# A filter by Fourier transform with a two-layer network behind it: the exchange between partition quarters by copy and add, arrays read back 32 steps ahead, tables loaded in another order

## Chip, cores and metric

The kernel runs on one core of one Trainium2 chip. The metric is the device time of one execution in microseconds; lower is better.

## What is computed

```python
X = np.fft.rfft(x, axis=1)                       # x: 8 x 3008 x 256, float32
Y = X * (filt_r + 1j * filt_i)[None]             # filters: 1505 x 256
y = np.fft.irfft(Y, n=3008, axis=1)
h = y.reshape(24064, 256) @ w_in                 # 256 x 2048
g = np.maximum(h, 0) + alpha * np.minimum(h, 0)  # alpha: 2048
out = g @ w_out                                  # 2048 x 256, float32
```

## The kernel before

**The work.** Each of the eight batches is filtered along its 3008 rows, and each row of the result goes through the network. The transform of 3008 points is done as 94 x 32 by matmuls with constant tables, in fp16. For batch b (class `Fft`) the pieces are:

- `piece_a` (L148), eight of them: the 94-point transform of a quarter tile of x (`xs`), evicted by ScalarE (ACT) to `asb`. `save_a` (L159) writes `asb` to `a_dram`.
- `turn_a` (L163): reads `a_dram` back as `at`, with the other index on the partitions (the "array" of the change). There is one `at`.
- `piece_b` (L172), six: the 32-point transform into `psF`. Its partitions hold, in quarters of 32, real and imaginary parts. The product with the complex filter is made by two multiplies on VectorE (DVE): `ww` is the product with the filter whose quarters are exchanged and signed (`filts_s`), `uu` that with the plain one (`filt_s`). Then `ww` of the neighbouring quarter has to be added to `uu`: four DMAs on GpSimd's (POOL's) queue with `accum_op=add`, one for each quarter (L189), which is the exchange.
- `piece_c` (L192), six: the inverse 32-point transform of `uu`, evicted by ACT to `v`. After every second one `turn_c` (L207) writes a third of `v` to `v_dram`, and the last one reads it back as `zt` in four DMAs.
- `pair_d` (L235), eight: the inverse 94-point transform into `yT`, the network's input.

The network runs over 48 blocks of 512 rows (four of 384), each in 16 steps. A step j does `up(j)`: 128 of the 2048 hidden units, two matmuls; after every odd j ACT evicts two of them to `gtb` (L458), DVE forms the negative part (L461), and after every fourth DVE adds it (L463, 128 x 2048). In the same step `prev.down(j)` does a sixteenth of the block before's second product (L480). So the loop has 768 steps, and the first block has no `down`.

**The order is written by hand.** `plan` maps a step to functions, which are issued ahead of that step's `up`. `plan_fft` (L494) takes for each batch the steps of its `piece_a`, `turn_a`, x loads, `piece_b`, `piece_c` and `pair_d`. For batches three to seven the steps count from p = 96 (b - 1): the last `piece_a` at p - 48 or p - 50, `turn_a` at p - 20, `piece_b` at p + 2, p + 14, ..., p + 62, `piece_c` at p + 14 to p + 74, `pair_d` from p + 91. Each engine takes its instructions in this order. SyncE's (SP's) queue carries the saves, the reads back and the output stores, POOL's the x loads and the exchange.

**Buffers.** `uu` has three, `ww` two, `psF` one of two PSUM banks, `hps` and `op` two each.

**Batch 0** is done ahead of the loop by class `First` (L253), without a way through DRAM: transposes on TensorE (PE) instead. Its filter rows for the first piece stand in `fst`, loaded by SP; the other filters are loaded by POOL. Tables are `twf`, `twi`, `twx` (three parts of the constants), `wf1`, `wi3` and the signs `sgn`. Matmuls of the identity (`warm`) fill PE's idle time there. Of batch 0's four groups of 752 rows the first is finished ahead of the loop, the other three in its first 30 steps (`piece_t`, a transposition into `zt`, and `pair_d`).

Of the kernel before, what the change touches and what calls it, by code (L numbers as in the profile page):

```python
# [9 lines left out]
FP16 = mybir.dt.float16  # L10
# [3 lines left out]
N1 = 94  # L14
N2 = 32
NK = 24
D = 256
# [4 lines left out]
OP = mybir.AluOpType  # L22
# [28 lines left out]
def kernel(  # L51
# [22 lines left out]
    p_uw = ctx.enter_context(tc.tile_pool(name="p_uw", bufs=2))  # L74
# [33 lines left out]

    def load_x(b, c):
        xs = p_x.tile([N1, 8 * D], FP16, name="xs")  # L110
        for r in (slice(0, 48), slice(48, N1)) if b else (slice(0, N1),):
            nc.gpsimd.dma_start(out=xs[r], in_=xrow(b, c)[r])  # L112
        return xs

    def load_filt(eng, dst, ha, hb):
        n = hb - ha
        for i, src in enumerate((filt_r, filt_i)):
            for e in range(2):
                q = 64 * e + 32 * i
# [18 lines left out]
    class Fft:  # L138
# [30 lines left out]
                        out=self.at[q : q + N2, ka:kb],  # L169
                        in_=a_dram[self.b, r + ka : r + kb].rearrange("k s d -> s k d"))  # L170

        def piece_b(self, q):  # L172
            psf = banks(False)
            for h in range(2):
                for par in range(2):
                    r = slice(64 * par, 64 * par + 64)
                    for e in range(2):
                        k = 4 * q + 2 * h + e
                        nc.tensor.matmul(psf[64 * e : 64 * e + 64, par, 256 * h : 256 * h + 256],  # L179
                                         twf_s[r, k], self.at[r, k], start=True, stop=True)  # L180
            px = psf.rearrange("p r (h d) -> p r h d", h=2)
            uu = p_uw.tile([128, 2, 2, D], FP16, name="uu", bufs=3)
            ww = p_uw.tile([128, 2, 2, D], FP16, name="ww")
            fs, f = (t[:, 2 * q : 2 * q + 2].rearrange("p h r d -> p r h d") for t in (filts_s, filt_s))
            nc.vector.tensor_mul(ww, px, fs)  # L185
            nc.vector.tensor_mul(uu, px, f)  # L186
            for o in range(0, 128, 32):
                i = o ^ 32
                nc.gpsimd.dma_start(out=uu[o : o + 32], in_=ww[i : i + 32], accum_op=OP.add)  # L189
            self.uw[q] = uu  # L190

        def piece_c(self, q):  # L192
            if q == 0:
                self.v = p_fft.tile([128, NK, D], FP16, name="v")
                self.zt = p_fft.tile([96, N2, D], FP16, name="zt")
            u = self.uw.pop(q)
            ps = psH.tile([128, 2, 512], FP32, name="hps")
            for h in range(2):
                for e in range(2):
                    r = slice(64 * e, 64 * e + 64)  # L200
                    for par in range(2):
                        nc.tensor.matmul(ps[64 * par : 64 * par + 64, e, 256 * h : 256 * h + 256],  # L202
                                         twi_s[r, 4 * q + 2 * h + par], u[r, par, h], start=True, stop=True)
            on_act(self.v[:, 4 * q : 4 * q + 4].rearrange("p (h e) d -> p e h d", e=2),
                   ps.rearrange("p e (h d) -> p e h d", h=2))
# [134 lines left out]
    def tables(eng, names, ka, kb):  # L340
        for n, t in (("twf", twf_s), ("twi", twi_s), ("twx", twx_s)):
            if n in names:
                eng.dma_start(out=t[:, ka:kb], in_=consts[n].ap()[:, ka:kb])

    xc = {(0, c): load_x(0, c) for c in range(4)}
    f0 = First()
    tables(nc.sync, ("twf",), 0, 8)
    nc.sync.dma_start(out=al16, in_=moe_alpha.rearrange("(j p) -> j p", p=128))
    nc.sync.dma_start(out=id32, in_=id32_d.ap())
    nc.sync.dma_start(out=sgn_s, in_=sgn_d.ap())  # L350
    nc.sync.dma_start(out=wf1_s, in_=consts["wf1"].ap())
    nc.sync.dma_start(out=wi3_s, in_=consts["wi3"].ap())
    load_filt(nc.gpsimd, filt_s, 1, 4)
    load_filt(nc.gpsimd, filt_s, 4, 8)
    load_filt(nc.gpsimd, filt_s, 8, 12)
# [9 lines left out]
    def warm(n, kind="o"):  # L365
        pw = bank(kind)
        for _ in range(n):
            nc.tensor.matmul(pw[:, 0:128], id16, id16, start=True, stop=True)
# [22 lines left out]
    for kp in range(0, 12, 2):  # L391
        if kp < 10:
            f0.piece_b(kp + 2)
            f0.piece_b(kp + 3)
        f0.piece_c(kp)
        f0.piece_c(kp + 1)
        f0.keep_c(kp, both if kp == 10 else (on_act, on_act))
        if kp < 6:
            f0.turn_at(kp + 6, 2, on_act)
        elif kp < 10:  # L400
            warm(4, "f")
# [6 lines left out]
    warm(8, "f")  # L408
# [82 lines left out]
    def put(step, fn, *args):  # L491
        plan.setdefault(step, []).append((fn, args))

    def plan_fft(b, a_at, ta, quarters, x_at, b_at, c_at, d_at):  # L494
# [12 lines left out]
        for q in range(6):  # L507
            put(b_at[q], f.piece_b, q)
        for q in range(6):
            put(c_at[q], f.piece_c, q)  # L510
            front.add(c_at[q])
            if q % 2 == 1:
                put(c_at[q] + 1, f.turn_c, q // 2)
        for i in range(8):
            put(d_at[i], f.pair_d, i, on_act)

    for g, ts, ds in ((1, (1, 3), (6, 8)), (2, (12, 14), (17, 19)), (3, (22, 24), (27, 29))):
        for i in range(2):
            put(ts[i], f0.piece_t, 2 * g + i, both[i])
            put(ds[i], f0.pair_d, 2 * g + i, both[i])  # L520
# [7 lines left out]
    def d_steps(p):  # L528
        return [p + t for t in (91, 93, 104, 108, 116, 120, 140, 152)]

    plan_fft(1, (8, 10, 12, 14, 16, 18, 20, 22), 24, 4, (12, 16, 20, 24), (32, 38, 46, 52, 58, 64),
             (46, 52, 58, 64, 70, 76), (90, 92, 98, 101, 106, 116, 136, 146))
    plan_fft(2, (54, 60, 66, 72, 80, 84, 88, 94), 97, 4, (62, 74, 86, 96), range(110, 170, 10),
             range(120, 180, 10), d_steps(96))
    for b in range(3, NB):
        p = 96 * (b - 1)
        a_at = (10, 16, 22, 28, 32, 38, 42, 48) if b == 3 else (6, 10, 18, 22, 30, 34, 42, 46)
# [53 lines left out]
```

## Time and profile before

| | |
|---|---|
| median of 3 runs | 813.55 us (811.96 to 815.87) |
| the profiled execution | 813.39 us, span 811.6 us |
| mean granted clock of PE | 0.976 |
| busy PE / DVE / ACT / POOL | 777.0 / 576.3 / 582.6 / 185.0 us |
| DMA traffic | 100.67 MB, mean 124 GB/s |

The span is the time from the first to the last instruction of the profiled execution; 1.8 us lie around it. PE is TensorE's matmuls, PEld its weight loads. A row of instructions in order of time has the start and the length in us, then the engine, the line of the kernel, the operation, out<-in with shapes and the count, and in brackets the engine's idle time just before and what ended it. A row of waits has the waiting engine and line, what it waited for, and then the sum in us, the number and the longest. L245 and L248 are the helpers `on_act` and `on_dve`, which evict for many pieces, so they are told apart by the tiles.

### The profile page before, as it was taken

The page shows a single profiled execution, that of the slowest core. Times are in us where ns is not written, and L with a number is a line of the kernel's source. Part 1 is how long each engine was busy: PE and PEld are TensorE (multiplying, and loading weights), DVE is VectorE, ACT ScalarE, POOL GpSimd, SP SyncE. Part 2 cuts the span into 40 slices and gives each one's busy share as a digit, 9 for nine tenths or more (in the row PEclk, how much of TensorE's full clock was granted, in tenths as well). Part 3 has the DMA queues.
Part 4 walks back from the last instruction along what each step waited for, and adds up shares of the span by engine and source line. Part 5 has one row for each costly group of instructions (what it writes and reads, how often), then busy time and mean ns, then how long its engine had stood idle before and what let it go on. Part 6 is the DMA issues. An engine that isn't in the chain of part 4 may idle for free.

```text
span 811.6 us, 16322 instructions
## 1 busy us (share of the span) xinstructions
PE 777.0 (96%) x6497; PEld 521.0 (64%) x6497; DVE 576.3 (71%) x1079; ACT 582.6 (72%) x667; POOL 185.0 (23%) x267
## 2 busy tenths in 40 slices
PE   6788999999999999899999999989999999999998
PEld 5555667665665666666666666756666666676666
DVE  3667886677765787677776778658776887767664
ACT  2587688877765877588776887668877677676764
POOL 5421450143302431033311243013130322100000
PEclk7699999999998999999999999999999999999999
DMA  8988588677594764957658665765449444531111
GB/s 157 196 193 187 120 157 208 178 127 140 97 186 97 133 146 80 200 85 144 129 110 161 123 127 122 155 122 101 103 74 194 83 76 87 110 86 34 40 40 53
DMA packets 97325, 100.67 MB, mean 124 GB/s; under 512 B 11216, under 2 KB 82400, under 8 KB 97056
## 3 DMA queue, kind: packets, MB, share of 16 engines
q1 hardware_dynamic: 80368, 70.25, 34.4%
q0 software_dynamic: 16880, 29.38, 26.4%
q8 instruction: 51, 0.84, 0.4%
q14 instruction: 26, 0.21, 0.1%
HBM read 55.28 MB, written 46.66 MB: 126 GB/s over the span
## 4 chain that ended last, share of the span: by engine, by line
PE 73%; DMA 16%; SPq 3%; ACT 3%; DVE 2%; POOL 1%; issue 1%; DVEq 0%; ACTq 0%; POOLq 0%
PE hps L449 33%; PE op L480 33%; DMA at<-a_dram 8%; DMA xs<-in_x_dram 4%; PE hps L155 2%; PE psF L224 2%; PE psF L179 2%; SPq L168 2%; DMA v_dram<-v 1%; DMA uu<-ww 1%; PE hps L202 1%; ACT gtb L458 1%; SPq L219 1%; DMA filt_s<-in_filt_i_dram 1%; DMA win_s<-in_moe_w_in_dram 1%
## 5 line engine op out<-in xcount | busy, mean ns | idle before, releaser
L458 ACT ACTIVATE gtb<-hps 128x1024 f16<-128x1024 f32 (+1 forms) x384 | 386.0, 1005 | 156.1 <-PE hps L449 154.2
L449 PE MATMUL hps<-yT,win_s 128*128 128x512 f16 (+1 forms) x1536 | 438.1, 377 | 2.5 <-ACT gtb L458 1.3
L480 PE MATMUL op<-wout_s,gtb 128*128 128x256 f16 x3008 | 438.8, 274 | 0.1
L480 PEld LDWEIGHTS <-gtb 128*128 128x128 f16 x3008 | 295.0, 98 | 171.9 <-issue 4.5
L461 DVE TENSOR_SCALAR m<-gtb,alm_s 128x512 f16<-128x512 f16 (+1 forms) x768 | 233.1, 347 | 186.5 <-ACT gtb L458 185.3
L463 DVE TENSOR_TENSOR gtb<-gtb,m 128x2048 f16<-128x2048 f16 (+1 forms) x192 | 231.1, 1203 | 10.4 <-PE hps L449 0.5
L189 POOL DMA_DIRECT2D uu<-ww x168 | 134.2, 1199 | 418.0 <-PE hps L449 179.3
L449 PEld LDWEIGHTS <-win_s 128*128 128x128 f16 x1536 | 143.3, 98 | 62.9 <-issue 16.4
L245 ACT ACTIVATE asb<-hps 96x1024 f16<-96x1024 f32 x56 | 57.1, 1020 | 11.2 <-PE hps L155 11.0
L485 ACT ACTIVATE osb<-op 128x512 f32<-128x512 f32 (+1 forms) x97 | 56.2, 579 | 5.3 <-issue 2.8
L185 DVE TENSOR_TENSOR ww<-psF,filts_s 128x1024 f16<-128x1024 f32 x42 | 51.2, 1219 | 8.6 <-PE psF L179 8.6
L245 ACT ACTIVATE v<-hps 128x1024 f16<-128x1024 f32 x42 | 43.0, 1024 | 17.7 <-PE hps L202 17.5
L245 ACT ACTIVATE yT<-psF 128x752 f16<-128x752 f32 x59 | 47.0, 797 | 8.4 <-PE psF L224 8.3
L112 POOL DMA_DIRECT2D xs<-in_x_dram x60 | 37.1, 708 | 66.7 <-PE hps L155 57.1
L186 DVE TENSOR_TENSOR uu<-psF,filt_s 128x1024 f16<-128x1024 f32 x42 | 51.1, 1216 | 0.0
L155 PE MATMUL hps<-xs,wf_s 94*96 94x512 f16 x112 | 33.4, 379 | 0.1
L224 PE MATMUL psF<-wi_s,zt 96*128 96x94 f16 x500 | 31.4, 206 | 1.5 <-DVE zt L248 1.5
L179 PE MATMUL psF<-at,twf_s 64*64 64x256 f16 x336 | 19.7, 288 | 12.7 <-DMA at<-a_dram 12.7
L224 PEld LDWEIGHTS <-zt 96*128 96x128 f16 x512 | 29.1, 99 | 4.3 <-issue 2.3
L179 PEld LDWEIGHTS <-twf_s 64*64 64x64 f16 x336 | 6.9, 105 | 22.7 <-DMA at<-a_dram 12.5
L202 PE MATMUL hps<-uu,twi_s 64*64 64x256 f16 x336 | 17.4, 272 | 2.8 <-DMA uu<-ww 2.7
L293 DVE TENSOR_TENSOR uu<-hps,filt_s 128x1024 f16<-128x1024 f32 x11 | 12.8, 1219 | 4.2 <-PE hps L289 3.6
(58 smaller groups left out, 155.4 us busy)
## 6 DMA issues: line engine op xcount, KB each, us to landing
out_dram<-osb SPq DMA_DIRECT2D x160, 128.0 KB
a_dram<-asb SPq DMA_DIRECT2D x28, 384.0 KB
uu<-ww POOLq DMA_DIRECT2D x168, 64.0 KB, 3.4
v_dram<-v SPq DMA_DIRECT2D x84, 128.0 KB
zt<-v_dram SPq DMA_DIRECT2D x28, 384.0 KB
at<-a_dram SPq DMA_DIRECT2D x20, 384.0 KB
xs<-in_x_dram POOLq DMA_DIRECT2D x28, 192.0 KB, 4.4
xs<-in_x_dram POOLq DMA_DIRECT2D x28, 184.0 KB, 5.4
```

Of the source, the lines that this page charges most:

```text
L155: nc.tensor.matmul(ps[0:96, u], wf1_s, xs[:, o : o + 512], start=True, stop=True)
L185: nc.vector.tensor_mul(ww, px, fs)
L186: nc.vector.tensor_mul(uu, px, f)
L189: nc.gpsimd.dma_start(out=uu[o : o + 32], in_=ww[i : i + 32], accum_op=OP.add)
L224: nc.tensor.matmul(ps[:, m], self.zt[:, 8 * g + 4 * mh + m, dh * 128 : dh * 128 + 128], wi3_s, start=True, stop=True)
L245: nc.scalar.activation(o, i, AF.Copy)
L449: nc.tensor.matmul(self.hps[:, j % 2, 0:tn], win_s[:, kt, j * 128 : (j + 1) * 128], yT[:, kt, self.t0 : self.t0 + tn], start=(kt == 0), st ...
L458: nc.scalar.activation(g[:, 2 * i : 2 * i + 2], self.hps[:, :, 0:tn], AF.Copy)
L461: nc.vector.tensor_scalar(m[:, 2 * i + h], g[:, 2 * i + h], 0.0, a, OP.min, OP.mult)
L463: nc.vector.tensor_add(g, g, m)
L480: nc.tensor.matmul(self.op[:, si - s0], self.gts[k][:, 128 * si : 128 * si + 128], wout_s[:, k], start=(si == s0 and k == 0), stop=(si == ...
L485: nc.scalar.activation(osb[:, 0:m], self.op[:, 0:m], AF.Copy)
```

## The change

- **The exchange.** For batch one it stays. For batches two to seven the four POOL DMAs are plain copies of `ww` into a new tile `sw`, and a new piece `piece_s` adds `sw` to `uu` on DVE, seven steps (batch two) or eight steps (later ones) after `piece_b`.
- **The reads back.** `turn_a` of batches three to seven moves from p - 20 to p - 32. `piece_b` stays at p + 2 and after, so the reads are 34 steps ahead of the first one and about 32 ahead of the group of steps that begins at p. For batches one and two the whole plan is shifted: batch one's `piece_a` by four steps later, its `piece_b` from 32 to 36, its `piece_c` to 12 steps after each `piece_b`; batch two's `turn_a` from 97 to 92, its `piece_b` from 110 to 104 on.
- **Tables and loads ahead of the loop.** `fst` is the first load of SP; `twi` and `twx` of the first eight columns come ahead of the first loop. The later tables, `wi3`, `wf1` and `sgn` are loaded in that loop, held back by a small memset of `twf_s` on DVE after its sixth piece. The x tiles of batch 0 are loaded in halves.
- **Warm matmuls** are a quarter as many, each four times as wide.
- **Batch 0's groups.** Group one is done in halves in steps 0 to 9, in `op`'s buffers; groups two and three move a few steps later, the one evicted by DVE, the other by ACT.

```diff
     def load_x(b, c):
-        for r in (slice(0, 48), slice(48, N1)) if b else (slice(0, N1),):
+        for r in (slice(0, 48), slice(48, N1)) :
...
-        def piece_b(self, q):
+        def piece_b(self, q, direct):
...
+            sw = None if direct else p_uw.tile([128, 2, 2, D], FP16, name="sw")
...
             for o in range(0, 128, 32):
                 i = o ^ 32
-                nc.gpsimd.dma_start(out=uu[o : o + 32], in_=ww[i : i + 32], accum_op=OP.add)
-            self.uw[q] = uu
+                if direct:
+                    nc.gpsimd.dma_start(out=uu[o : o + 32], in_=ww[i : i + 32], accum_op=OP.add)
+                else:
+                    nc.gpsimd.dma_start(out=sw[o : o + 32], in_=ww[i : i + 32])
+            self.uw[q] = uu, sw
+
+        def piece_s(self, q):
+            uu, sw = self.uw[q]
+            nc.vector.tensor_add(uu, uu, sw)
...
+    load_filt(nc.sync, f0.fst, 0, 1)
     tables(nc.sync, ("twf",), 0, 8)
...
-    nc.sync.dma_start(out=sgn_s, in_=sgn_d.ap())
-    nc.sync.dma_start(out=wf1_s, in_=consts["wf1"].ap())
-    nc.sync.dma_start(out=wi3_s, in_=consts["wi3"].ap())
+    tables(nc.sync, ("twi", "twx"), 0, 8)
...
-            nc.tensor.matmul(pw[:, 0:128], id16, id16, start=True, stop=True)
-    warm(36)
+            nc.tensor.matmul(pw.rearrange("p (r c) -> p r c", r=4), id16,
+                             id16.unsqueeze(1).to_broadcast([128, 4, 128]), start=True, stop=True)
+    warm(9)
     for i in range(8):
...
-            warm((16, 8, 8, 8)[i // 2])
-        if i == 3:
-            nc.vector.memset(f0.fst[:, :, :, 0:1], 0.0)
-            load_filt(nc.sync, f0.fst, 0, 1)
-            tables(nc.sync, ("twi", "twx"), 0, 8)
+            warm((4, 2, 2, 2)[i // 2])
+        if i == 5:
+            nc.vector.memset(twf_s[:, 8:24, 0:1], 0.0)
             tables(nc.sync, ("twf", "twi", "twx"), 8, 24)
-        if i == 5:
+            nc.sync.dma_start(out=wi3_s, in_=consts["wi3"].ap())
+            nc.sync.dma_start(out=wf1_s, in_=consts["wf1"].ap())
+            nc.sync.dma_start(out=sgn_s, in_=sgn_d.ap())
...
         for q in range(6):
-            put(b_at[q], f.piece_b, q)
+            put(b_at[q], f.piece_b, q, not add)
+            if add:
+                put(b_at[q] + add, f.piece_s, q)
...
-    for g, ts, ds in ((1, (1, 3), (6, 8)), (2, (12, 14), (17, 19)), (3, (22, 24), (27, 29))):
+    for i in range(4):
+        put(i, f0.half_t, 4 + i, both[i % 2], "o")
+        put(6 + i, f0.half_d, 4 + (0, 2, 1, 3)[i], both[i % 2], "o")
+    for g, ts, ds, evict in ((2, (13, 15), (21, 23), on_dve), (3, (25, 27), (31, 33), on_act)):
...
-    plan_fft(1, (8, 10, 12, 14, 16, 18, 20, 22), 24, 4, (12, 16, 20, 24), (32, 38, 46, 52, 58, 64),
-             (46, 52, 58, 64, 70, 76), (90, 92, 98, 101, 106, 116, 136, 146))
-    plan_fft(2, (54, 60, 66, 72, 80, 84, 88, 94), 97, 4, (62, 74, 86, 96), range(110, 170, 10),
-             range(120, 180, 10), d_steps(96))
+    plan_fft(1, range(12, 28, 2), 28, 4, (17, 21, 25, 29), range(36, 72, 6), 0, range(48, 84, 6),
+             (91, 93, 98, 101, 106, 116, 136, 152))
+    plan_fft(2, (50, 56, 62, 68, 74, 80, 84, 88), 92, 4, (57, 69, 81, 89), (104, 114, 126, 136, 148, 158), 7,
+             (114, 126, 136, 148, 158, 170), d_steps(96))
...
-        plan_fft(b, a_at, p - 20, 1, [a_at[2 * c + 1] + 2 for c in range(4)],
-                 range(p + 2, p + 74, 12), range(p + 14, p + 86, 12), d_steps(p))
+        plan_fft(b, a_at, p - 32, 1, [a_at[2 * c + 1] + 2 for c in range(4)],
+                 range(p + 2, p + 74, 12), 8, range(p + 14, p + 86, 12), d_steps(p))
```

More of the change, by code (lines that the diff above doesn't have):

```diff
@@ L195, in piece_c @@
                 self.zt = p_fft.tile([96, N2, D], FP16, name="zt")
-            u = self.uw.pop(q)
+            u, _ = self.uw.pop(q)
             ps = psH.tile([128, 2, 512], FP32, name="hps")
@@ L400 @@
         elif kp < 10:
-            warm(4, "f")
+            warm(1, "f")
     nc.gpsimd.dma_start(out=filt_s[:, 0:1], in_=f0.fst)
@@ L407 @@
         nc.gpsimd.dma_start(out=filt_s[o : o + 32], in_=filt_s[o - 32 : o])
-    warm(8, "f")
+    warm(2, "f")
     for i, (evict, kind) in enumerate(((on_act, "o"), (on_dve, "o"), (on_act, "f"), (on_dve, "h"))):
@@ L492, in put, with plan_fft @@
         plan.setdefault(step, []).append((fn, args))
-    def plan_fft(b, a_at, ta, quarters, x_at, b_at, c_at, d_at):
+    def plan_fft(b, a_at, ta, quarters, x_at, b_at, add, c_at, d_at):
         f = Fft(b)
@@ L515, in plan_fft @@
             put(d_at[i], f.pair_d, i, on_act)
-    for g, ts, ds in ((1, (1, 3), (6, 8)), (2, (12, 14), (17, 19)), (3, (22, 24), (27, 29))):
+    for i in range(4):
+        put(i, f0.half_t, 4 + i, both[i % 2], "o")
+        put(6 + i, f0.half_d, 4 + (0, 2, 1, 3)[i], both[i % 2], "o")
+    for g, ts, ds, evict in ((2, (13, 15), (21, 23), on_dve), (3, (25, 27), (31, 33), on_act)):
         for i in range(2):
-            put(ts[i], f0.piece_t, 2 * g + i, both[i])
-            put(ds[i], f0.pair_d, 2 * g + i, both[i])
+            put(ts[i], f0.piece_t, 2 * g + i, evict)
+            put(ds[i], f0.pair_d, 2 * g + i, evict)
     def neg(ha, hb):
@@ L529, in d_steps @@
         return [p + t for t in (91, 93, 104, 108, 116, 120, 140, 152)]
-    plan_fft(1, (8, 10, 12, 14, 16, 18, 20, 22), 24, 4, (12, 16, 20, 24), (32, 38, 46, 52, 58, 64),
-             (46, 52, 58, 64, 70, 76), (90, 92, 98, 101, 106, 116, 136, 146))
-    plan_fft(2, (54, 60, 66, 72, 80, 84, 88, 94), 97, 4, (62, 74, 86, 96), range(110, 170, 10),
-             range(120, 180, 10), d_steps(96))
+    plan_fft(1, range(12, 28, 2), 28, 4, (17, 21, 25, 29), range(36, 72, 6), 0, range(48, 84, 6),
+             (91, 93, 98, 101, 106, 116, 136, 152))
+    plan_fft(2, (50, 56, 62, 68, 74, 80, 84, 88), 92, 4, (57, 69, 81, 89), (104, 114, 126, 136, 148, 158), 7,
+             (114, 126, 136, 148, 158, 170), d_steps(96))
     for b in range(3, NB):
         p = 96 * (b - 1)
-        a_at = (10, 16, 22, 28, 32, 38, 42, 48) if b == 3 else (6, 10, 18, 22, 30, 34, 42, 46)
+        a_at = (10, 16, 22, 28, 34, 36, 44, 48) if b == 3 else (6, 10, 18, 22, 30, 34, 42, 46)
         a_at = [p - 96 + t for t in a_at]
-        plan_fft(b, a_at, p - 20, 1, [a_at[2 * c + 1] + 2 for c in range(4)],
-                 range(p + 2, p + 74, 12), range(p + 14, p + 86, 12), d_steps(p))
+        plan_fft(b, a_at, p - 32, 1, [a_at[2 * c + 1] + 2 for c in range(4)],
+                 range(p + 2, p + 74, 12), 8, range(p + 14, p + 86, 12), d_steps(p))
     prev = None
```

## Prediction

> **What bounds the kernel now.** I read the page first, then the list of waits, then PE's instructions in order of time at the waits, then windows of 16 us around them.
>
> ```profile
> PE 777.0 (96%) x6497; PEld 521.0 (64%) x6497; DVE 576.3 (71%) x1079; ACT 582.6 (72%) x667; POOL 185.0 (23%) x267
> ...
> PEclk7699999999998999999999999999999999999999
> ```
>
> PE is busy 96% of the span, DVE and ACT some 70%. So PE sets the time, and what can be won is the time in which PE waits, and the time in which it runs with a low granted clock. The clock row (tenths, 40 slices of 20 us) shows such slices at the start and one near 244 us. The list of waits names the waiters:
>
> ```profile
> DVE m L461 <- ACT gtb L458: 185.3, 202, 3.1
> ...
> PE psF L179 <- DMA at<-a_dram: 12.7, 8, 3.0
> ...
> PE hps L202 <- DMA uu<-ww: 2.7, 2, 1.9
> ```
>
> PE's longest waits are those of `piece_b` (L179) for `at`, the read back of the first transform's array; then those of `piece_c` (L202) for `uu`, the exchange of the partition quarters. The 185.3 us of DVE are slack: DVE idles there until ACT has written the next `gtb`. PE's instructions in order of time (start, length, then in brackets the idle time before) put the L179 waits at one place of each batch, the first `piece_b`:
>
> ```profile
> 80.35 0.41 PE L179 MATMUL psF<-at,twf_s 64*64 64x256 f16 x6 [0.68 <-DMA at<-a_dram]
> ...
> 242.22 0.30 PE L179 MATMUL psF<-at,twf_s 64*64 64x256 f16 x2 [0.25 <-DMA at<-a_dram]
> ...
> 245.12 0.64 PE L179 MATMUL psF<-at,twf_s 64*64 64x256 f16 x6 [2.60 <-DMA at<-a_dram]
> ...
> 343.10 0.57 PE L179 MATMUL psF<-at,twf_s 64*64 64x256 f16 x6 [2.98 <-DMA at<-a_dram]
> ...
> 439.37 0.41 PE L179 MATMUL psF<-at,twf_s 64*64 64x256 f16 x6 [1.75 <-DMA at<-a_dram]
> ...
> 534.52 0.64 PE L179 MATMUL psF<-at,twf_s 64*64 64x256 f16 x6 [3.00 <-DMA at<-a_dram]
> ...
> 629.91 0.41 PE L179 MATMUL psF<-at,twf_s 64*64 64x256 f16 x6 [0.97 <-DMA at<-a_dram]
> ```
>
> The windows around these places (length, then busy time of PE, PEld, DVE, ACT, POOL with counts, granted clock, DMA share, GB/s), with one from the first block of the main loop:
>
> ```profile
> 48.00:64.00 16.00, 14.26 (x102) 8.31 (x102) 13.08 (x26) 14.83 (x16) 6.12 (x12) 1.00 0.86 207
> 240.00:256.00 16.00, 13.15 (x81) 7.58 (x79) 8.36 (x16) 7.57 (x10) 3.14 (x4) 0.79 0.56 99
> 336.00:352.00 16.00, 13.00 (x89) 7.70 (x86) 9.53 (x20) 8.62 (x11) 3.15 (x4) 0.89 0.75 131
> 432.00:448.00 16.00, 14.26 (x115) 9.61 (x114) 11.29 (x20) 10.77 (x13) 3.14 (x4) 1.00 0.76 130
> 528.00:544.00 16.00, 12.97 (x88) 7.91 (x86) 9.68 (x18) 8.83 (x11) 3.14 (x4) 0.89 0.71 122
> 624.00:640.00 16.00, 15.03 (x125) 10.04 (x123) 12.01 (x22) 10.42 (x14) 3.14 (x4) 1.00 0.76 136
> ```
>
> In three of the five the clock fell as well, and 81 to 89 matmuls ran instead of 115 to 125. So a wait here costs twice: the wait itself, and PE's slow time behind it.
>
> The sum below is made against the profiled execution, 813.39 us for a span of 811.6; the median of the runs shown is 813.55, so nothing has to be shifted.
>
> **The reads of `at`, batches three to seven.** They are issued at step p - 32 instead of p - 20, and the first `piece_b` stays at p + 2. The waits are 0.25 + 2.60 + 2.98 + 1.75 + 3.00 + 0.97 = 11.6 us (PE's idle time in the five windows gives 2.85 + 3.00 + 1.74 + 3.03 + 0.97 = 11.6 too). The clock costs (0.21 + 0.11 + 0.11) x 16 = 6.9 us of full-speed time. Together 18.5 us; I take off 1.0, since some of the slow time lies inside the waits and is counted twice: 17.5. Do twelve steps suffice? Where the reads stand now, in SP's queue and in the chain of waits:
>
> ```profile
> 223.25 3.85 DMA v_dram<-v
> ...
> 231.15 13.93 DMA at<-a_dram
> ```
>
> ```profile
> 228.94 9.16 SPq L168 DMA_DIRECT2D at<-a_dram  x4
> ```
>
> SP issues them right behind `turn_c(2)`, which at step p - 21 writes `v_dram` and reads `zt` back, so the `at` reads share the DMA engines with the `zt` reads and end at 245.1, 16 us after the first issue. Twelve steps earlier they stand ahead of `turn_c(2)`. A step is about 1 us (768 steps lie within the span of 811.6), so the shift is 11 us or a little more against a longest wait of 3.0: 8 us in hand. Two things can hold SP: the array must be written (last `save_a` at p - 48 or p - 50, 16 steps before), and `at` must be free (`piece_b(5)` of the batch before at p - 34, two steps before). Neither reaches the next use. Queued behind the four issues on SP are the output stores and, eleven steps later, `turn_c(2)`; SP was held 9.16 us by these issues with the `zt` reads in front, and eleven steps are about as long, so `zt` is not later than now. What comes next in turn is the exchange of `piece_b(5)`, at p - 34, which now runs beside the reads; see the next part. Bounds: 11.6 (the waits alone) to 18.5.
>
> At this place the Trainium skill speaks for a smaller gain: "TensorE: Matmul & The Clock Gate", section "HAM oscillation", gives as the rule that only idle gaps over about 3.4 us take the clock away. By it none of these waits costs clock, the term would be 11.6 and the time 6 us later. The trace differs: after waits of 2.6 to 3.0 us the windows show 0.79 and 0.89, after 1.75 and 0.97 us 1.00.
>
> **Copy and add instead of the accumulating DMA, batches two to seven.** Removed is the wait of the four POOL issues for the second multiply. Added are 36 `tensor_add` of 128x1024 on DVE, each waiting for four landings, and everything on DVE queues behind that wait. One steady piece in order of time on DVE, and POOL's four issues:
>
> ```profile
> 274.34 1.22 DVE L185 TENSOR_TENSOR ww<-psF,filts_s 128x1024 f16<-128x1024 f32 x1
> ...
> 281.90 0.61 DVE L461 TENSOR_SCALAR m<-gtb,alm_s 128x512 f16<-128x512 f16 x2
> 284.01 0.62 DVE L461 TENSOR_SCALAR m<-gtb,alm_s 128x512 f16<-128x512 f16 x2 [1.50 <-ACT gtb L458]
> ...
> 286.33 1.22 DVE L185 TENSOR_TENSOR ww<-psF,filts_s 128x1024 f16<-128x1024 f32 x1
> ```
>
> ```profile
> 276.98 3.18 POOL L189 DMA_DIRECT2D uu<-ww  x4 [5.88 <-DVE uu L186]
> ```
>
> The window around it, an L463 for the length of an add, and the time from issue to landing of the 168 exchange DMAs:
>
> ```profile
> 272.00:288.00 16.00, 16.00 (x134) 10.31 (x132) 13.04 (x24) 13.08 (x16) 4.26 (x6) 1.00 0.82 176
> ```
>
> ```profile
> L463 DVE TENSOR_TENSOR gtb<-gtb,m 128x2048 f16<-128x2048 f16 (+1 forms) x192 | 231.1, 1203 | 10.4 <-PE hps L449 0.5
> ```
>
> ```profile
> DMA to landing us min/median/max: 2.4/3.4/6.1
> ```
>
> The add is half an L463: about 0.65 us, 36 of them 23 us of DVE. POOL now waits for the second multiply, which starts when the first ends and is as long; without that wait it can start 1.1 us sooner, at 275.9. Four issues take 3.18, the last begins near 278.2 and lands 3.4 later, at 281.6. The add is put eight steps behind `piece_b`, where j is 2, 6, 10 or 14, that is between the first and the second pair of L461 of a group: here at 282.5, where DVE idles 1.50 us. So it finds its data and fits into the gap, and is done at 283.2; `piece_c` follows the next `piece_b`, near 286, 2.8 us later. Cost nothing, the cover being that gap. Without it a piece costs the add, at most 0.65 x 36 = 23 us if DVE were the bound, which at 71% it is not. For batch two the add stands seven steps behind and `piece_c` ten to twelve. Now all its `piece_c` stand ten behind and waited 2.7 us in two of them; the copy starts 1.1 us sooner and gives 0.65 back. I take half of the 2.7 as saved, 1.4; bounds -2 and +2.7. For the sixth piece of each batch, beside the reads of `at`, a landing of 6.1 us would bring the add to 284.3 and its end to 285, still ahead of `piece_c`. Nothing is taken for it.
>
> **First block of the loop.** In 48 to 64 us ACT is busy 14.83 of 16: there ACT is the bound, since no down projection runs yet.
>
> ```profile
> L245 ACT ACTIVATE asb<-hps 96x1024 f16<-96x1024 f32 x56 | 57.1, 1020 | 11.2 <-PE hps L155 11.0
> ...
> L245 ACT ACTIVATE yT<-psF 128x752 f16<-128x752 f32 x59 | 47.0, 797 | 8.4 <-PE psF L224 8.3
> ...
> L245 ACT ACTIVATE zt<-psF 96x1024 f16<-96x1024 f32 x3 | 3.0, 1017 | 2.0 <-PE psF L324 2.0
> ...
> L245 ACT ACTIVATE zt<-op 96x512 f16<-96x512 f32 x1 | 0.6, 593 | 1.0 <-PE op L324 1.0
> ...
> L245 ACT ACTIVATE yT<-op 128x376 f16<-128x376 f32 x1 | 0.5, 484 | 0.1
> ```
>
> Out of steps 0 to 15 on ACT go two `asb` (batch one's `piece_a` starts at 12 instead of 8), two `zt` and one `yT`: 2.04 + 2.03 + 0.80 = 4.9 us. In come two half `zt` and two half `yT`: 2.2. Net 2.7 us less. DVE, busy 13.1 of the 16 already, takes over group two's `zt` and may become the bound itself; the lower bound is then less than half of this, 1.2 us. Block two gets two `asb` more, beside PE work that is as long. Batch one's `at` wait (0.68 above) keeps its distance of ten steps and stays. In favour of more: group two's evictions no longer alternate, and DVE's waits there go. I take 3.0; bounds 1.2 to 4.5.
>
> **Before the loop.** The single filter rows (`fst`) and `twi`, `twx` now load ahead of the first x tiles' end, and x comes in eight DMAs instead of four. The longer warm matmuls have the same columns in a quarter of the instructions.
>
> ```profile
> fst<-in_filt_r_dram SPq DMA_DIRECT2D x4, 32.0 KB
> ...
> twi_s<-c_twi SPq DMA_DIRECT2D x1, 128.0 KB
> ```
>
> ```profile
> PE psF L368 <- issue: 2.3, 1, 2.3
> ```
>
> With `filt_i` and `twx` these are 8 x 32 + 2 x 128 = 512 KB; at the 207 GB/s of the window above 2.5 us of the DMA engines, which x may lose at most, and nothing if they fit beside it. On the other side 69 pairs of PE instructions go; PE's 2.3 us without any recorded wait may be instructions that came late, and may go or move. The ends are +2.5 and -2.3; I take 0, the middle. But one call of `warm`, the last, keeps its count of 4 and so gets four times as long, and stands right ahead of the last pieces before the loop:
>
> ```profile
> 40.89 0.63 PE L368 MATMUL op<-id 128*128 128x128 f16 x4
> ...
> 41.31 0.52 PE L224 MATMUL hps<-wi_s,zt 96*128 96x94 f16 x4
> ```
>
> Four take the 0.42 us between these starts, so sixteen take 1.7. The pieces behind them waited for `zt` only little, so up to 1.3 us is added, and nothing where the eviction of `zt` hides it: +0.8.
>
> The sum: 813.4 - 17.5 - 1.4 - 3.0 + 0.8 = 792.3 us.
>
> **The rivals.** First, half of the gain comes back: the next arrival at the head of a batch is late. For it: the exchange of the sixth piece now meets four 384 KB reads, and `zt` waits behind them on SP. Against it: the 2.8 us and the 8 us in hand. If each of five batches gives back 2 us, the time is 802.
>
> Second, and slower: the add blocks DVE. A piece has 12.0 us of DVE time (274.34 to 286.33), of which (16 - 13.04) / 16, 2.2 us, are idle by the window around it, so 1.5 us is left behind the add. Landing L us after the last issue, the add waits L - 4.3 (278.2 + L against 282.5), and DVE falls behind by L - 5.8 in each of 36 pieces. The gain of 21.1 is eaten from L = 6.4 on; at L = 7 the time is 792.3 + 36 x 1.2 = 835. For it: 6.1 occurs today. Against it: that is the largest of 168, the median is 3.4, and only one piece in six runs beside the reads.
>
> Third, the change doesn't do what it says: SP is held at the earlier place and the reads start no sooner. Then only 3.6 us of the other parts are left: 810. For it: SP's queue is in order, and the reads wait for a `piece_b` only two steps before. Against it: 30 steps remain after that.
>
> **How the numbers follow.** A measurement of this kernel tells about 0.5% from no change, here 4 us. The forecast has 0.64, with 785 to 797 as its own range from the bounds of the start (+3.8, -2.3), of block one (1.2 to 4.5) and batch two; the first rival has 0.19, the second 0.11, the third 0.06. The range takes in the forecast and the first rival, 785 to 806. Faster is the forecast and the first rival, 0.83; the third lies at the edge and stands for no change, 0.06; slower is the second, 0.11.
>
> **What would show it.** Right: no L179 wait for `at` after 200 us and a clock of 1.00 in the windows that follow; the new add's group with 36 of about 0.65 us and little idle time before them for the landing of `sw`; L461's idle time down by about 23 us; the first block shorter by 3 us. Wrong: L202 waiting for the add, L224 waiting for `zt` at the head of a batch, DVE idle ahead of the add by more than 1.5 us a piece, or a first step of the loop that begins more than 2.5 us later than now.

## The result, and the profile after

| | median | runs |
|---|---|---|
| before | 812.91 us | 811.96 to 815.87 (4) |
| changed | 793.15 us | 792.41 to 793.86 (4) |

The ratio is 0.9751, 95% interval [0.9723, 0.9779]: faster by 2.5%. The forecast was 792.3 us. The profiled execution of the changed kernel took 792.9 us for a span of 791.1, at a mean granted clock of 0.989 (0.976 before).

In the changed kernel lines have moved down by eight: ACT's `gtb` is L466, DVE's negative part L469, `up` L457, `down` L488, the matmuls of `piece_c` L210 (L202 before) and those of `pair_d` L232 (L224 before). The multiplies are L186 (`ww`) and L187 (`uu`), the accumulating exchange L191, the copy L193, the add L198. Busy time and the clock row on its page, and the rows of the groups that the change touches:

```profile
PE 768.3 (97%) x6428; PEld 512.9 (65%) x6428; DVE 596.7 (75%) x1117; ACT 582.9 (74%) x669; POOL 142.9 (18%) x271
...
PEclk8799999999999999999999999999999999999999
...
L193 POOL DMA_DIRECT2D sw<-ww x144 | 70.8, 500 | 385.1 <-DVE ww L186 382.3
...
L198 DVE TENSOR_TENSOR uu<-uu,sw 128x1024 f16<-128x1024 f16 x36 | 24.6, 684 | 0.0
```

DVE has 20 us more to do and the kernel is 20 us faster. The add does not wait: no idle time stands before it (0.0 in its row). An exchange issue on POOL takes 0.50 us; the accumulating one took 1.20, as its row on the page of before shows:

```profile
L189 POOL DMA_DIRECT2D uu<-ww x168 | 134.2, 1199 | 418.0 <-PE hps L449 179.3
```

Then the changed kernel's list of waits, and the windows that stand against the five of before (length; busy PE, PEld, DVE, ACT, POOL; clock; DMA share; GB/s):

```profile
PE psF L232 <- DVE uu L187: 3.1, 3, 1.2
...
PE psF L179 <- DMA at<-a_dram: 1.3, 2, 0.7
```

```profile
240.00:256.00 16.00, 16.00 (x139) 10.54 (x137) 13.63 (x24) 12.77 (x15) 3.37 (x7) 1.00 0.46 99
...
528.00:544.00 16.00, 16.00 (x144) 10.48 (x142) 13.79 (x23) 13.92 (x17) 2.52 (x6) 1.00 0.35 94
```

The waits for `at` fell from 12.7 us to 1.3, both of those left lie in batch two, and PE is busy throughout at full clock in these two windows, where it ran at 0.79 and 0.89.

Where the time went can be read from the starts of ACT's `gtb` evictions. Those of steps 0 and 96, then 192 and 672, first in the trace of before, then in the changed kernel's:

```profile
45.43 1.01 ACT L458 ACTIVATE gtb<-hps 128x1024 f16<-128x1024 f32 x1
...
144.82 1.02 ACT L458 ACTIVATE gtb<-hps 128x1024 f16<-128x1024 f32 x1 [0.26 <-PE hps L449]
...
241.58 1.02 ACT L458 ACTIVATE gtb<-hps 128x1024 f16<-128x1024 f32 x1 [0.22 <-PE hps L449]
...
718.05 1.02 ACT L458 ACTIVATE gtb<-hps 128x1024 f16<-128x1024 f32 x1 [0.33 <-PE hps L449]
```

```profile
43.53 1.02 ACT L466 ACTIVATE gtb<-hps 128x1024 f16<-128x1024 f32 x1 [0.65 <-PE hps L457]
...
141.13 1.02 ACT L466 ACTIVATE gtb<-hps 128x1024 f16<-128x1024 f32 x1 [0.33 <-PE hps L457]
...
240.08 1.02 ACT L466 ACTIVATE gtb<-hps 128x1024 f16<-128x1024 f32 x1 [0.22 <-PE hps L457]
...
697.48 1.02 ACT L466 ACTIVATE gtb<-hps 128x1024 f16<-128x1024 f32 x1 [0.33 <-PE hps L457]
```

| stretch | before | changed | difference | predicted |
|---|---|---|---|---|
| start to step 0 | 45.43 | 43.53 | -1.9 | +0.8 |
| step 0 to 96 | 99.39 | 97.60 | -1.8 | -3.0 |
| step 96 to 192 (beside it, batch two) | 96.76 | 98.95 | +2.2 | -1.4 |
| step 192 to 672 (batches three to seven) | 476.47 | 457.40 | -19.1 | -17.5 |

So the total agrees to a microsecond, three terms do not, and what made the fourth had still to be found. The experiments use the same four points. Each stretch is read from one profiled execution, and 31 runs of the kernel before lie between 806.49 and 818.66 us; so a difference of 2 or 3 us in one stretch counts for little unless a wait in the trace accounts for it.

### The profile page after: what moved, and what is told of

Same layout as the page of the kernel before. It is cut to its first block, busy times and chain, and to the rows that moved or that the text cites. A ratio compares the mean times of both kernels' runs of the same rounds, so it can differ in the third digit from the quotient of the medians.

```text
span 791.1 us, 16237 instructions
## 1 busy us (share of the span) xinstructions
PE 768.3 (97%) x6428; PEld 512.9 (65%) x6428; DVE 596.7 (75%) x1117; ACT 582.9 (74%) x669; POOL 142.9 (18%) x271
## 4 chain that ended last, share of the span: by engine, by line
PE 90%; ACT 3%; DMA 2%; DVE 2%; issue 1%; SPq 1%; POOL 1%; DVEq 0%; ACTq 0%; POOLq 0%
PE hps L457 40%; PE op L488 40%; PE hps L155 3%; PE psF L232 2%; PE psF L179 2%; ACT gtb L466 2%; PE hps L210 1%; DMA xs<-in_x_dram 1%; DMA filt_s<-in_filt_r_dram 1%; DVE uu L301 1%; SPq L168 1%; ACT asb L253 1%; POOL xs L112 0%; PE op L316 0%; PE psF L332 0%
## 5 line engine op out<-in xcount | busy, mean ns | idle before, releaser
L466 ACT ACTIVATE gtb<-hps 128x1024 f16<-128x1024 f32 (+1 forms) x384 | 385.6, 1005 | 137.8 <-PE hps L457 136.8
L457 PE MATMUL hps<-yT,win_s 128*128 128x512 f16 (+1 forms) x1536 | 435.1, 375 | 2.0 <-ACT gtb L466 1.5
L488 PE MATMUL op<-wout_s,gtb 128*128 128x256 f16 x3008 | 435.8, 273 | 0.1
L488 PEld LDWEIGHTS <-gtb 128*128 128x128 f16 x3008 | 294.0, 98 | 168.3 <-issue 0.4
L469 DVE TENSOR_SCALAR m<-gtb,alm_s 128x512 f16<-128x512 f16 (+1 forms) x768 | 233.0, 346 | 154.0 <-ACT gtb L466 153.1
L457 PEld LDWEIGHTS <-win_s 128*128 128x128 f16 x1536 | 142.6, 98 | 60.1 <-issue 15.4
L193 POOL DMA_DIRECT2D sw<-ww x144 | 70.8, 500 | 385.1 <-DVE ww L186 382.3
L253 ACT ACTIVATE asb<-hps 96x1024 f16<-96x1024 f32 x56 | 57.1, 1019 | 11.7 <-PE hps L155 11.4
L186 DVE TENSOR_TENSOR ww<-psF,filts_s 128x1024 f16<-128x1024 f32 x42 | 51.1, 1217 | 0.0
L187 DVE TENSOR_TENSOR uu<-psF,filt_s 128x1024 f16<-128x1024 f32 x42 | 51.0, 1214 | 0.0
L232 PEld LDWEIGHTS <-zt 96*128 96x128 f16 x512 | 28.9, 99 | 8.4 <-issue 3.2
L232 PE MATMUL psF<-wi_s,zt 96*128 96x94 f16 x484 | 30.2, 205 | 3.2 <-DVE uu L187 3.1
L198 DVE TENSOR_TENSOR uu<-uu,sw 128x1024 f16<-128x1024 f16 x36 | 24.6, 684 | 0.0
L191 POOL DMA_DIRECT2D uu<-ww x24 | 19.3, 1221 | 26.2 <-DVE uu L187 21.9
L179 PE MATMUL psF<-at,twf_s 64*64 64x256 f16 x336 | 17.8, 281 | 2.4 <-DMA at<-a_dram 1.3
L210 PE MATMUL hps<-uu,twi_s 64*64 64x256 f16 x336 | 16.5, 271 | 0.0
```

Source lines behind the costliest of these rows:

```text
L193: nc.gpsimd.dma_start(out=sw[o : o + 32], in_=ww[i : i + 32])
L232: nc.tensor.matmul(ps[:, m], self.zt[:, 8 * g + 4 * mh + m, dh * 128 : dh * 128 + 128], wi3_s, start=True, stop=True)
L253: nc.scalar.activation(o, i, AF.Copy)
L457: nc.tensor.matmul(self.hps[:, j % 2, 0:tn], win_s[:, kt, j * 128 : (j + 1) * 128], yT[:, kt, self.t0 : self.t0 + tn], start=(kt == 0), st ...
L466: nc.scalar.activation(g[:, 2 * i : 2 * i + 2], self.hps[:, :, 0:tn], AF.Copy)
L469: nc.vector.tensor_scalar(m[:, 2 * i + h], g[:, 2 * i + h], 0.0, a, OP.min, OP.mult)
```

## The experiments

Two accounts of the 19 us in batches three to seven were open. By the prediction's account the earlier reads earn it, and the exchange by copy is neutral. By the other, a piece of the first rival, earlier reads only move the collision: they meet the exchange of the sixth `piece_b`, and it is the lighter exchange that lets them pass. A ratio is always to runs of the kernel before that were taken beside it. The table has the stretches beside batch two and batches three to seven, and five waits, one for the reads of each of the batches three to seven. Batch three's reads at p - 32 meet batch two's sixth piece, so that wait lies in the stretch before step 192. The sections follow.

| kernel | reads | exchange | step 96 to 192 | step 192 to 672 | PE's five waits |
|---|---|---|---|---|---|
| before | p - 20 | accumulate | 96.76 | 476.47 | `at`, 0.97 to 3.00 |
| `before_reads32` | p - 32 | accumulate | 102.07 | 472.97 | `uu`, 1.63 to 3.99 |
| `before_copyadd` | p - 20 | copy and add | 92.95 | 474.20 | `at`, 0.84 to 3.47 |
| changed | p - 32 | copy and add | 98.95 | 457.40 | none |
| `after_accum` | p - 32 | accumulate | 103.09 | 471.05 | `uu`, 0.80 to 3.12 |
| `after_reads20` | p - 20 | copy and add | 100.31 | 476.94 | `at`, 0.98 to 3.90 |

**The reads alone.** In the kernel before:

```diff
-        plan_fft(b, a_at, p - 20, 1, ...
+        plan_fft(b, a_at, p - 32, 1, ...
```

> The kernel before with one edit: the reads of at for batches three to seven at step p - 32 instead of p - 20; the accumulating exchange stays. Theory of the lead: the reads alone make the gain behind step 192, about 19 us of the 20; expected 794, no L179 wait for at after 230 us, clock 1.00 there. Rival theory of the exchange: the accumulating DMAs of the sixth piece meet the reads, land late, and piece_c (L202) waits for uu; then at most half of the gain is seen, 803 or more.

Measured: 812.23 us, 1.0006 [0.9972, 1.004]. The waits for `at` are gone, but others of the same size came. In its list of waits, and three of the five in order of time:

```profile
PE hps L202 <- DMA uu<-ww: 15.8, 7, 4.0
...
PE psF L179 <- DMA at<-a_dram: 1.3, 2, 0.6
```

```profile
223.44 1.05 PE L202 MATMUL hps<-uu,twi_s 64*64 64x256 f16 x8 [3.99 <-DMA uu<-ww]
...
321.45 0.41 PE L202 MATMUL hps<-uu,twi_s 64*64 64x256 f16 x6 [2.07 <-DMA uu<-ww]
...
608.13 0.41 PE L202 MATMUL hps<-uu,twi_s 64*64 64x256 f16 x6 [3.16 <-DMA uu<-ww]
```

Each is the `piece_c` of the sixth piece. POOL issues that piece's four DMAs from 311.51 (for the wait at 321.45), SP the four reads from 313.43:

```profile
311.51 3.12 POOL L189 DMA_DIRECT2D uu<-ww  x4 [8.09 <-DVE uu L186]
```

```profile
313.43 4.13 SPq L168 DMA_DIRECT2D at<-a_dram  x4
```

```profile
DMA to landing us min/median/max: 2.9/5.0/8.4
```

The last line is the landing of these four exchange DMAs: up to 8.4 us, where the largest of all 168 was 6.1 before. PE's gain at `at` is paid back at `uu` in full: the waits for `at` fell by 11.4 us, those for `uu` rose by 13.1. From step 192 on the kernel is 3.5 us shorter, but the stretch before, with the wait of 3.99 us, is 5.3 longer. The account that the reads earn the gain by themselves has fallen.

**The changed kernel with one part undone.** First the reads back at p - 20, then `add` set to 0 for all batches, so that every exchange accumulates:

```diff
-        plan_fft(b, a_at, p - 32, 1, ...
+        plan_fft(b, a_at, p - 20, 1, ...
```

> The changed kernel with the reads of batches three to seven back at p - 20. Theory of the lead: the five waits of 1 to 3 us and the low clock behind three of them come back, 793 + 19 = 812. Rival theory of the exchange: the shorter exchange made the gain, and the time stays at 793 to 797.

```diff
-    (104, 114, 126, 136, 148, 158), 7,
+    (104, 114, 126, 136, 148, 158), 0,
-    range(p + 2, p + 74, 12), 8, range(...
+    range(p + 2, p + 74, 12), 0, range(...
```

> The changed kernel with the accumulating exchange in all batches, no sw and no add; the plan is otherwise that of after. Theory of the lead: the exchange has room enough in batches three to seven; only batch two, with three piece_c ten steps behind, may wait 1 to 3 us for uu, so 793 to 796. Rival theory of the exchange: the sixth piece of each batch now meets the reads and L202 waits for uu in each of them, 800 or more.

Measured: 810.51 us, 0.9983 [0.9955, 1.0011], and 811.29 us, 0.9999 [0.9975, 1.0022]. Each undoing alone takes back all that can be told from no change. With the old reads the waits for `at` and the lower clock return; with the accumulating exchange `piece_c` waits again for the sixth piece's `uu`, and DMAs land up to 9.1 us after their issue. From the two lists of waits:

```profile
PE psF L179 <- DMA at<-a_dram: 11.6, 7, 3.9
```

```profile
PE hps L210 <- DMA uu<-ww: 11.4, 6, 3.1
```

**The copy alone.** The kernel before with copy and add as in the changed kernel, its plan otherwise kept:

```diff
-  range(110, 170, 10), ...              # batch two
+  range(110, 170, 10), 7, ...
-  range(p + 2, p + 74, 12), ...         # batches three to seven
+  range(p + 2, p + 74, 12), 8, ...
```

> The kernel before with one edit: copy to sw and an add on DVE for batches two to seven (seven steps behind piece_b in batch two, eight in the later ones); reads at p - 20. Theory of the lead: only the two L202 waits of batch two, 2.7 us together, can go: 811 to 813. Rival theory of the exchange: 803 or less. If the add blocked DVE, slower than 813.

Measured: 806.97 us, 0.995 [0.9923, 0.9976], between the two forecasts. The waits for `at` at the heads stay. Batch two's two waits for `uu` go, and its stretch falls from 96.76 to 92.95 us. So the copy alone earns 3.8 us there and 2.3 in batches three to seven. The reads alone earned 3.5 in batches three to seven and lost 5.3 before them. Both together earn 19.1 in batches three to seven. The gain belongs to the pair.

**Only the sixth piece.** In the changed kernel the first five pieces accumulate as before, only the sixth is copied:

```diff
-            put(b_at[q], f.piece_b, q, not add)
-            if add:
+            put(b_at[q], f.piece_b, q, not add or q < 5)
+            if add and q == 5:
```

> The changed kernel with the plain copy and the add in the sixth piece alone of batches two to seven; the first five pieces accumulate by DMA. Theory of the sixth piece (only its exchange meets the reads): 793 to 796, no L210 wait in batches three to seven, at most some in batch two. Rival theory of the whole exchange (five accumulating pieces hold up POOL or the DMA engines for others as well): 800 or more.

Measured: 793.62 us, 0.977 [0.974, 0.98], with 457.40 us from step 192 to 672: the changed kernel's time, to the hundredth, with 6 pieces copied in the place of 36. What the copy is needed for is the one piece of each batch that meets the reads.

**Lighter, or merely earlier?** A copy of `ww` can start before the second multiply, 1.1 us sooner, which by itself gives it a head start over the reads. In this kernel `uu` is multiplied first, so that the copy starts as late as the accumulation did:

```diff
-            nc.vector.tensor_mul(ww, px, fs)
             nc.vector.tensor_mul(uu, px, f)
+            nc.vector.tensor_mul(ww, px, fs)
```

> The changed kernel with the two multiplies of piece_b exchanged, so that the copies start 1.1 us later, as the accumulating ones do. Theory of the head start: the copies of the sixth piece meet the reads, the add and with it L210 come late in five batches, 800 or more. Theory of the lighter exchange (issues of 0.5 instead of 1.2 us, plain copies): the copies still land within 4.5 us and no L210 wait appears, 793 to 795.

Measured: 797.63 us, 0.9818 [0.9764, 0.9871], and again 457.40 us from step 192 to 672; the 2.6 us above the forecast lie in batch two. The head start is the one of the accumulating case, 1.92 us (POOL's issues and the landing of these four copies):

```profile
309.54 2.12 POOL L193 DMA_DIRECT2D sw<-ww  x4 [9.27 <-DVE ww L187]
```

```profile
DMA to landing us min/median/max: 2.2/2.5/2.9
```

SP's first read starts at 311.46 here. So at the same head start the copies land within 2.9 us where the accumulating DMAs took 8.4. In the next three meetings, batches four to six, the reads come 0.94 to 1.93 us behind the copies, which land within 2.8 to 4.8 us (the forecast had 4.5). In the ten meetings of `before_reads32` and `after_accum` the slowest accumulating DMA took 7.1 to 9.1. In batches three to six the copy wins by landing quickly beside the same reads, and not by its earlier start. Why the accumulating DMA suffers more from the reads is not shown.

The earlier start has its worth all the same. Batch two's sixth piece meets batch three's reads, which in this kernel begin 0.50 us behind its copies (2.08 in the changed kernel). The landing of these four copies, and the `piece_c` that waits for the add:

```profile
DMA to landing us min/median/max: 2.4/3.8/7.0
```

```profile
221.69 0.57 PE L210 MATMUL hps<-uu,twi_s 64*64 64x256 f16 x8 [2.25 <-DVE uu L198]
```

The stretch of batch two is 4.6 us longer here (103.59), with a clock of 0.89 from 144 to 160 and from 216 to 232 us, where the changed kernel has 1.00.

**Other places for the reads.** With the accumulating exchange, is there a place that suits? At p - 27 and p - 24 in the kernel before:

> The kernel before with one edit: the reads of batches three to seven at p - 27, five steps later than in the change; the accumulating exchange stays. Theory of the collision (the accumulating exchange of the sixth piece, which lands about seven steps behind its piece_b at p - 34, must be over before the reads fill the DMA engines): at p - 27 most of it has landed, so the five L202 waits of 1.6 to 4 us are gone or under 1 us and no L179 wait comes instead; 794 to 798. Rival theory of the accumulate (it is too slow in itself wherever the reads stand ahead of turn_c): the L202 waits stay near 2 us with the low clock, 805 to 812.

> The kernel before with one edit: the reads of batches three to seven at p - 24, which on SP's queue is behind the output stores of step p - 25, so that they start about 8 us later than at p - 27 or p - 32, and still ahead of turn_c(2). Theory of the collision: the accumulating DMAs have landed, the L202 waits of batches three to seven go; instead zt, three steps behind, comes late and L224 waits 1 to 3 us in each: 803 to 812. Theory of the slow accumulate: the L202 waits stay. If there is a place for the reads that hurts neither: 795 to 798.

The first, 813.83 us, 1.002 [0.9983, 1.0058], tells little: nothing stands on SP's queue between the two places, so the reads began 1.92 us behind POOL's issues, as at p - 32 (315.69 against 313.77), and its waits for `uu` stay, up to 4.01 us. A step in the plan is a place in a queue, not a time. The second stands behind the output stores, and its reads began 7.9 us behind POOL's (320.51 against 312.58). It took 815.93 us, 1.0045 [1.002, 1.007]: the waits for `uu` in batches three to seven are gone, and the list of waits has a third kind:

```profile
PE psF L224 <- DMA zt<-v_dram: 14.6, 5, 5.0
```

At p - 20 the reads are late themselves, at p - 24 they hold up `zt` behind them, at p - 32 they hit the exchange: 11.6 to 14.6 us of waiting move from one victim to the next. The same was tried in the changed kernel, at p - 22:

> The changed kernel with the reads of batches three to seven at p - 22, that is only two steps earlier than before, but ahead of turn_c(2) on SP's queue. Theory of the place in the queue: L179 no longer waits for at, and the zt reads, now behind them, are late by several us for the pair_d at p - 5: new L232 waits, 3 us and more in each of five batches with the clock, 808 to 820. Theory of the plain lead: the waits shrink by the two steps, 3 us to 1 and less, 796 to 799.

Measured: 815.42 us, 1.0042 [1.0011, 1.0072]. No `piece_b` of batches three to seven waits, but `zt` is late in all five, 2.51 to 3.61 us each (14.4 together). So two steps already bring `at` in time. More are needed to get the reads out of the way of `zt`, whose `turn_c(2)` stands at p - 21: in the kernel before `zt` was late at p - 24 and no longer at p - 27. The least lead that serves with the copy was not looked for.

**Batch two, mended.** Where the shifted plan loses 2.2 us, PE's instructions in order of time show:

```profile
148.26 0.41 PE L179 MATMUL psF<-at,twf_s 64*64 64x256 f16 x6 [0.61 <-DMA at<-a_dram]
...
151.77 0.49 PE L232 MATMUL psF<-wi_s,zt 96*128 96x94 f16 x8 [1.15 <-DVE uu L187]
...
163.09 0.51 PE L232 MATMUL psF<-wi_s,zt 96*128 96x94 f16 x8 [1.19 <-DVE uu L187]
```

Batch one's `pair_d` (106, 116, 136, 152) stands two or four steps behind batch two's `piece_b` (104, 114, 136, 148) or in one step with it, and takes `psF`, of which there is one buffer, before the two multiplies of that `piece_b` have read it. This kernel parts them, starts batch two two steps later, and puts the last warm call back to its old work:

```diff
-             (91, 93, 98, 101, 106, 116, 136, 152))
+             (91, 93, 98, 101, 110, 120, 131, 142))
-             (104, 114, 126, 136, 148, 158), 7,
-             (114, 126, 136, 148, 158, 170), d_steps(96))
+             (106, 116, 126, 136, 148, 158), 7,
+             (116, 126, 136, 148, 158, 170), d_steps(96))
...
-    warm(4)
+    warm(1)
```

> The changed kernel with three edits: the four later pair_d of batch one away from the piece_b of batch two (110, 120, 131, 142 instead of 106, 116, 136, 152); the first two piece_b and the first piece_c of batch two two steps later (106, 116; 116); the last warm call with 1 instead of 4. Expected: the L232 waits for the second multiply (3.1 us), the L179 waits for at and for the eviction (2.4 us) and 1.2 us ahead of the loop go: 787 to 790. If these waits were only the place where time shows that is lost anyway, 792 to 794.

Measured: 787.99 us (787.27 to 789.06, 6 runs), 0.9703 [0.9663, 0.9743], the fastest of all. The stretch of batch two fell from 98.95 to 93.76 us, 5.2 of the 5.4 us by which its span (785.7) is shorter than the changed kernel's. Its waits, against 3.1 and 1.3 above:

```profile
PE psF L179 <- DMA at<-a_dram: 0.5, 2, 0.3
...
PE psF L232 <- DVE uu L187: 0.3, 1, 0.3
```

The two edits to the plan were not tried apart. With the old plan and the copy, in `before_copyadd`, the stretch was 92.95 us; so the mended plan gets back what the shifted one had lost, and no more. The changed kernel also moves three `piece_a` of batch three by two steps in this stretch (32, 38, 42 became 34, 36, 44, counted from p - 96); no run undid that.

**Ahead of the loop.** Why did the changed kernel start 1.9 us sooner, and not 0.8 later? Two candidates: fewer PE instructions to issue, or the order of the loads. In the changed kernel, first narrow warm matmuls, four times as many; then the old order of the loads:

> The changed kernel with the warm matmuls in 128 columns, four times as many, so that PE has its 69 pairs of instructions more ahead of the loop, as before, at the same columns. Theory of late instructions: PE's wait without a recorded releaser of 1.5 to 3 us ahead of L297 comes back and the first L466 starts near 45 us instead of 43.5: 794 to 796. If the order of the loads made the gain ahead of the loop: first L466 near 43.5, 793.

> The changed kernel with the loads ahead of and in the first loop in the order of before (x tiles whole, fst and the tables behind the fourth piece_a, wf1, wi3 and sgn at the start). Theory of late instructions: no change, first L466 near 43.5 us, 793. Theory of the loads: first L466 near 45 us, 795; or below 43, if the earlier tables cost x time.

Measured: 794.55 us, 0.9786 [0.975, 0.9821], first `gtb` at 40.62; and 794.18 us, 0.9789 [0.9754, 0.9824], first `gtb` at 43.06. Six profiles of the changed code ahead of the loop begin between 41.65 and 44.08 (mean 43.4), five of the old between 44.50 and 45.43 (mean 45.0). So neither undoing brings the later start back, and the narrow warms even start sooner, which they lose again by step 96 (141.36 against 141.13). A part of the scatter is the granted clock, as a window shows for the changed kernel, then for the narrow warms:

```profile
32.00:44.00 12.00, 10.29 (x137) 7.09 (x125) 5.83 (x8) 4.90 (x9) 2.15 (x4) 0.72 1.22 206
```

```profile
32.00:44.00 12.00, 10.61 (x172) 8.43 (x165) 7.71 (x14) 7.70 (x13) 2.17 (x5) 1.00 1.24 204
```

The difference is worth 3.4 us of full-speed time, more than the 2.9 by which the second starts sooner. The clock alone does not explain the 1.6 us, for `before_copyadd`, with the old code, has 0.72 in this window as well and begins at 45.10. With one profile of each undoing in such a scatter neither candidate is shown, and neither is excluded; undoing both at once was not tried. The 1.6 us stay without a cause.

## Why the prediction was right, and where it was not

**The reads, -17.5 against -19.1.** The size was right: waits and clock together, and the windows confirm it, with 16.00 of 16 busy at 1.00. The owner was wrong. The step that failed is "Nothing is taken for it", the exchange of the sixth piece beside the reads. It was argued with a landing of 6.1 us. For an accumulating exchange the runs show 7.1 to 9.1, and with it the first rival's mechanism returns all of the gain (1.0006). It failed to decide here only because copies beside the reads land sooner, within 3.2 us in the changed kernel. The prediction put the copy down as "Cost nothing" and never asked what the reads would do without it, so it did not see that its largest term needed the part that it had set down as neutral.

At the clock the Trainium skill, "TensorE: Matmul & The Clock Gate", section "HAM oscillation", would have let no wait below about 3.4 us cost clock. Most of the waits moved by these experiments are shorter, and the trace differs again: with the old reads in the changed kernel a wait of 1.62 us comes with a clock of 0.89 in its window, while 1.63 us in `before_reads32` comes with 1.00. In `after_reads22` even 3.61 us comes with 1.00. So the prediction's "a wait here costs twice" held for most of the longer waits, not for each. The first two rows are of `after_reads20`, the last two of `after_reads22`:

```profile
435.74 0.41 PE L179 MATMUL psF<-at,twf_s 64*64 64x256 f16 x6 [1.62 <-DMA at<-a_dram]
```

```profile
432.00:448.00 16.00, 14.38 (x102) 8.94 (x100) 10.30 (x18) 9.80 (x12) 3.00 (x6) 0.89 0.49 109
```

```profile
626.49 0.51 PE L232 MATMUL psF<-wi_s,zt 96*128 96x94 f16 x8 [3.61 <-DMA zt<-v_dram]
```

```profile
624.00:640.00 16.00, 13.51 (x115) 9.19 (x116) 9.64 (x18) 9.34 (x11) 1.97 (x4) 1.00 0.59 161
```

**`zt`, and the eight microseconds in hand.** Right for p - 32, and for the reason given: no L232 wait for `zt` there. At p - 22 and p - 24, nearer, the reads stand in its way.

**Copy and add.** The add cost nothing, in the gap named: 36 at 0.684 us (0.65 predicted), and DVE's idle time at the negative part fell from 186.5 to 154.0 us, 8 us more than the add's 24.6; the kernel being shorter by 20 us has a share in that. POOL's four issues were taken over as 3.18 us; as copies they take 1.96. The second rival never came near: of 144 copies the largest landing is 4.4 us, and it begins to cost at 5.8.

**Batch two, -1.4 against +2.2.** The exchange's share was even too small: copied alone it gave -3.8 us. The sum took the new plan to be the old one in other steps, and looked at `uu` alone. `psF`, which `piece_b` and `pair_d` share, was in no step of it. The mended plan shows the price of the shift, 5.2 us, in which the sharing and the later start of batch two are not told apart.

**The first block, -3.0 against -1.8.** The first block of the loop fell by 1.4 us (16.1 to 14.7), the second by 0.8, and later ones up to step 96 lost 0.4. That is near the lower bound of 1.2, whose reason was that DVE takes over evictions; no run took this apart.

**Ahead of the loop, +0.8 against -1.9.** The direction was wrong, but not by the term that was worked out. The last warm call did get longer (1.7 us), first in the changed, then in the mended kernel, which has the old length:

```profile
38.59 1.91 PE L375 MATMUL op<-id 128*128 128x512 f16 x4
```

```profile
39.23 0.63 PE L375 MATMUL op<-id 128*128 128x512 f16 x1
```

From the start of this call to the first `gtb` it is 4.94 us in the one and 3.72 in the other, so the longer call costs the 1.2 us or so that were expected. The step that failed is the 0 taken for all that stands ahead of the call: it begins 2.3 us sooner than in the kernel before (38.59 against 40.89). Why is open, as said above. The four errors, -2.7, +1.2, +3.6 and -1.6 us, sum to 0.5; that the total agrees so closely is luck.

## What to carry to other kernels

A transfer moved earlier in a queue is not free where it lands: list every transfer that it will overtake or overlap, and size each by a landing under that load, not by today's. When two parts of a change are costed one by one, ask of each what it is worth without the other; here the reads alone earned nothing (1.0006), the copy alone 0.5%, and the whole change 2.5%. When steps of a hand-written plan move, follow the shared accumulator banks as well as the data.

## What was not expected of the hardware

- An accumulating DMA on POOL's queue occupies it for 1.20 us, a plain copy of the same 64 KB for 0.50. Their median landings are 3.4 and 2.5 us. Beside four 384 KB reads that began 1.9 us behind them the accumulating ones took up to 8.4 to 9.1 us, the copies 2.8 to 2.9. With reads only 0.50 us behind a copy took 7.0, the most in any run.
- The clock after a PE wait has no sharp threshold in these windows: 1.62 us was followed by 0.89, but 1.63, 1.75 and 3.61 us by 1.00.
